# Padding three small SBUF tiles so that matmul operands start at multiples of 512 bytes

## The chip, the cores and the metric

The kernel runs on one core of one Trainium2 chip. The metric is the device time of one execution in microseconds (us). Three runs of the kernel before took 2649.01, 2649.41 and 2650.83 us; their median is 2649.41 us.

## What is computed

The inputs are float32. An attention stage pools `kv` (2 x 384 x 32 x 128) over 4 x 4 blocks, multiplies the pooled rows by `w_sr`, and uses the result (768 rows for each of the 2 batches) as keys and as values for 12288 queries of width 128 in each batch. Two MLPs follow on all 24576 rows, each 128 -> 2048 -> 128.

```
kv_flat = mean_4x4(kv) @ w_sr                  # (2, 768, 128); k = v = kv_flat
s = (q @ k.T) / sqrt(128); s = s - max(s)
x = exp(s) / (sum(exp(s)) + 1e-09) @ v         # (2, 12288, 128) -> 24576 rows
h = x @ moe_w_in;   x = (h * cos(h)) @ moe_w_out                       # MLP 0
h = x @ moe2_w_in;  x = (h / (1 + exp(-1.702 * h))) @ moe2_w_out       # MLP 1
```

## The kernel before

**Products in three parts.** Float32 operands are split in two float32r parts each, a high one and a low one, and a product is made of three matmuls: high by low, high by high, low by high. For the MLPs the helper `mm3` (L107 to L110) issues the three, one line each:

```
def mm3(o, wh, wl, xh, xl, start, stop):
    nc.tensor.matmul(o, wh, xl, start=start, stop=False)      # L108
    nc.tensor.matmul(o, wh, xh, start=False, stop=False)      # L109
    nc.tensor.matmul(o, wl, xh, start=False, stop=stop)       # L110
```

The first operand is the stationary one, which TensorE loads with a weight load of 128 columns (512 bytes of each partition); the second is the moving one, 512 columns (2048 bytes of each partition). Every matmul has a weight load of its own.

**Units and steps.** The 24576 rows are cut in 48 units of 512. In an MLP a unit takes 8 steps. A step expands two blocks of 128 hidden features (`expanded`: six matmuls, moving `xs`, stationary `wi`, into a PSUM tile `w`), makes them non-linear on ScalarE and VectorE (L590 to L603), splits the result into the two parts of `gs` (`split`, L606 to L616), and adds it into the output (`project`: six matmuls, moving `gs`, stationary `wo`, into the PSUM bank `a`, three steps later). Both MLPs together issue 48 x 2 x 8 x 12 = 9216 matmuls of 512 columns.

**Attention.** The first 12 units go through `attn_step`: scores (L388: moving `kT`, stationary `qT`, 384 columns), transposes (L413), and the product with the values (L443: stationary `vN`, 256 columns). The moving operand of L443 is a tile that `pT_place` puts in turn in the place `ph`, in the place `pl`, and in the space of `gs`. The other 36 units go through `burst_step` between the MLP steps: scores at L476 (24 matmuls of 384 columns a unit), and the values at L538 (18 matmuls of 512 columns a unit: stationary `vN`, moving `pl` and `ph`, in the same order of high and low parts as in `mm3`).

**Order of the work.** The order on every engine is written out by hand (`at(step, rank, ...)`, `run`, under `tc.manual_schedule()`). From about 196 us to 440 us only MLP 0 runs, for the first 11 units, and VectorE also prepares the weights of MLP 1 (`w_split`, L227 to L242). From about 490 us to 2350 us each period of 53.14 us holds one unit of MLP 1, one of attention and one of MLP 0. The rest is MLP 1 alone.

**Where tiles lie.** Tiles of a pool lie one behind the other along the partition in the order in which they are made, each rounded up to 32 bytes. Ahead of the first stand 16384 reserved bytes and four constants of 32 bytes, so that the first tile, `ident`, starts at byte 16512. Two tiles of the pool `cp` are much smaller than 512 bytes:

```
peak = cp.tile([P, 2 * B], F32, tag="peak", name="peak")          # L114: 16 bytes, takes 32
half_pi = cp.tile([P, 1], F32, tag="half_pi", name="half_pi")     # L650: 4 bytes, takes 32
```

All tiles made behind each of them in `cp`, and the pools behind `cp`, start 32 bytes further. Within a tile the slices that matmuls read begin at multiples of 512 bytes, so that every operand of a tile has its tile's remainder by 512. The next table gives these remainders, as the built program has them.

Of the kernel before, what the change touches and what calls it, by code (L numbers as in the profile page):

```python
# [11 lines left out]
F32 = mybir.dt.float32  # L12
# [7 lines left out]
P = 128  # L20
# [3 lines left out]
LAG = 3  # L24
T_LAG = 3
BLK = 32
GATE = 1.702
PV_CUTS = (0, 0, 6, 12, 18)
TWO_PI = 2.0 * math.pi
# [6 lines left out]
def tile_pooled_attention_two_mlps(  # L36
# [12 lines left out]
    B, N, C = q.shape  # L49
# [13 lines left out]
    scale = 1.0 / math.sqrt(C)  # L63
    NB, KB = UNIT // BLK, NK // BLK
    assert AHEAD < LEAD < UB and C == P and N % UNIT == 0 and KC * P == NK and HK % P == 0
    assert P // BLK == QT

    cp = ctx.enter_context(tc.tile_pool(name="cp", bufs=1))
# [3 lines left out]
    st = ctx.enter_context(tc.tile_pool(name="st", bufs=4))  # L72
    ps = ctx.enter_context(tc.tile_pool(name="ps", bufs=1, space=bass.MemoryType.PSUM))

    ident = cp.tile([P, P], F32, tag="ident", name="ident")
    make_identity(nc, ident)
    wsr = cp.tile([P, C], F32, tag="wsr", name="wsr")
# [26 lines left out]
    def f32(ap):  # L104
        return ap.bitcast(F32)
# [5 lines left out]


    pooled, staged = {}, {}
    peak = cp.tile([P, 2 * B], F32, tag="peak", name="peak")  # L114

    def kv_place(b, j):

# [197 lines left out]
    def token_blocks(ap, u, i):  # L315

        rows = ap[u * UNIT : (u + 1) * UNIT, i * BLK : (i + 1) * BLK]
        return rows.rearrange("(b j) c -> j b c", j=BLK)

    q_flat = q.rearrange("b n c -> (b n) c")  # L320

    def q_load(u):
# [3 lines left out]
        if u < LEAD:  # L326
            nc.sync.dma_start(t, tokens(q_flat, u))
            return
        t = t.rearrange("p j c -> p (j c)").rearrange("p (b c) -> p b c", c=BLK)
        for i in range(QT):  # L330
            nc.sync.dma_start(t[i * BLK : (i + 1) * BLK], token_blocks(q_flat, u, i))

# [244 lines left out]
    def mlp_step(s, m, u, p):  # L577
# [7 lines left out]
        def nonlinear():  # L585
            h = v["h"]
            g = v["g"] = fp.tile([P, 2, UNIT], F32, tag="f", name=f"g{m}_{u}_{p}")
            if m == 1:

                nc.scalar.activation(g, h, AF.Silu, scale=GATE)  # L590
                return
# [13 lines left out]
        def split():  # L605
            g = v["g"]  # L606
            gs = v["gs"] = gs_ring[turn_of[s] % 3]
            if m == 1:
                nc.scalar.activation(gs[:, 0], g, AF.Copy, scale=1.0 / GATE)  # L609
                nc.vector.scalar_tensor_tensor(  # L610
                    gs[:, 1], g, 1.0 / GATE, f32(gs[:, 0]), op0=ALU.mult, op1=ALU.subtract
                )
# [34 lines left out]
        for i in range(QT):  # L647
            nc.sync.dma_start(token_blocks(out, u, i), r[i * BLK : (i + 1) * BLK])

    half_pi = cp.tile([P, 1], F32, tag="half_pi", name="half_pi")  # L650


    steps = [(attn_step, u, t) for u in range(LEAD) for t in range(QT)]
# [179 lines left out]
```

## Time and profile before

| | before |
|---|---|
| median of three runs | 2649.41 us (2649.01 to 2650.83) |
| profiled execution, its own time | 2649.0 us |
| span from its first to its last instruction | 2647.1 us |
| TensorE (PE) busy | 2607.0 us, 98% of the span |
| VectorE (DVE), ScalarE (ACT), GpSimd (POOL) busy | 78%, 79%, 21% |
| mean granted clock of TensorE | 0.999 |

A matmul's duration in this profile reaches from its start to a modelled end, and the next matmul starts before that end. A busy share of 98% so does not say how fast matmuls follow one another; the distance between two starts says it. The chain of waits cuts its steps at those starts, and a piece of it with a count gives the distance directly.

### The profile page before, as it was taken

To read this page: it belongs to the slowest core of one execution; us is meant where nothing else is said; L and a number is where in the kernel's file an instruction comes from. 1 tells how busy PE (TensorE), PEld (TensorE's weight loads), DVE (VectorE), ACT (ScalarE), POOL (GpSimd) and SP (SyncE) were. 2 spreads that over 40 slices of the span, in tenths; PEclk is the share of its full clock that TensorE was granted. 3 is DMA by queue.
4 is the path that set the end of the run, shared out by engine and by line. 5 is a ranking of instruction groups with operands and counts; after the bars stand their busy time and mean duration, and the time that the engine had idled before them with its cause. 6 is when DMAs were issued, how large, how long until landed. Compare 5 with 4: busy or idle time off the path is not lost.

```text
span 2647.1 us, 32479 instructions
## 1 busy us (share of the span) xinstructions
PE 2607.0 (98%) x11832; PEld 2148.8 (81%) x11832; DVE 2059.2 (78%) x2297; ACT 2101.7 (79%) x2449; POOL 543.9 (21%) x430
## 2 busy tenths in 40 slices
PE   5999999999999999999999999999999999999998
PEld 5987877888888888888888888888888888888887
DVE  6989998878787878787878787878787878765444
ACT  4777788888888888888888888888888888877776
POOL 5842332112111211121111111121112111200000
PEclk9999999999999999999999999999999999999999
DMA  8210001211221122112211221122112211210000
GB/s 216 73 33 16 17 20 28 41 33 32 56 41 33 32 54 43 33 32 51 45 32 32 48 49 33 33 47 49 33 33 44 49 35 32 39 22 9 13 11 16
DMA packets 317434, 105.06 MB, mean 40 GB/s; under 512 B 188112, under 2 KB 309072, under 8 KB 317264
## 3 DMA queue, kind: packets, MB, share of 16 engines
q1 hardware_dynamic: 317264, 102.89, 19.7%
q8 instruction: 95, 1.56, 0.2%
q14 instruction: 75, 0.61, 0.1%
HBM read 33.62 MB, written 12.58 MB: 17 GB/s over the span
## 4 chain that ended last, share of the span: by engine, by line
PE 94%; DVE 4%; DMA 1%; ACT 0%; POOL 0%; issue 0%; SPq 0%; POOLq 0%; DVEq 0%; ACTq 0%
PE a L108 13%; PE w L108 13%; PE w L110 13%; PE w L109 13%; PE a L110 13%; PE a L109 13%; PE a L538 6%; PE w L476 6%; PE a L443 1%; PE w L388 1%; PE w L413 1%; DVE g L603 1%; DMA kv<-in_kv_dram 1%; DVE gs L616 1%; DVE wt L234 0%; DVE nm L395 0%
## 5 line engine op out<-in xcount | busy, mean ns | idle before, releaser
L610 DVE SCALAR_TENSOR_TENSOR gs<-g,gs 128x1024 fp32r<-128x1024 f32 x384 | 469.0, 1222 | 355.8 <-ACT gs L609 355.8
L108 PE MATMUL a<-gs,wo 128*128 128x512 f32 x1536 | 607.9, 396 | 1.2 <-DVE gs L616 0.7
L108 PE MATMUL w<-xs,wi 128*128 128x512 f32 x1536 | 607.6, 396 | 0.6 <-ACT e L489 0.6
L110 PE MATMUL a<-gs,wo 128*128 128x512 f32 x1536 | 607.5, 396 | 0.0
L109 PE MATMUL a<-gs,wo 128*128 128x512 f32 x1536 | 607.5, 395 | 0.0
L109 PE MATMUL w<-xs,wi 128*128 128x512 f32 x1536 | 607.4, 395 | 0.0
L110 PE MATMUL w<-xs,wi 128*128 128x512 f32 x1536 | 607.3, 395 | 0.0
L593 ACT ACTIVATE g<-w,half_pi 128x1024 f32<-128x1024 f32 x384 | 428.4, 1116 | 168.8 <-PE w L110 168.5
L590 ACT ACTIVATE g<-w 128x1024 f32<-128x1024 f32 x384 | 395.2, 1029 | 210.2 <-PE w L110 209.6
L603 DVE TENSOR_TENSOR g<-w,g 128x1024 f32<-128x1024 f32 x384 | 467.9, 1219 | 120.3 <-ACT g L593 116.4
L616 DVE TENSOR_TENSOR gs<-g,gs 128x1024 fp32r<-128x1024 f32 x368 | 451.1, 1226 | 38.3 <-ACT gs L614 36.7
L614 ACT ACTIVATE gs<-g 128x1024 fp32r<-128x1024 f32 x384 | 404.3, 1053 | 2.3 <-DVE g L603 2.3
L609 ACT ACTIVATE gs<-g 128x1024 fp32r<-128x1024 f32 x384 | 399.4, 1052 | 0.0
L377 POOL TENSOR_TENSOR xs<-x,xs 128x512 fp32r<-128x512 f32 x96 | 174.8, 1821 | 859.1 <-PE w L110 444.0
L108 PEld LDWEIGHTS a<-gs,wo 128*128 128x128 f32 x1536 | 288.5, 188 | 72.8 <-DVE gs L616 2.0
L108 PEld LDWEIGHTS w<-xs,wi 128*128 128x128 f32 x1536 | 288.6, 188 | 70.2 <-ACT e L489 0.9
L110 PEld LDWEIGHTS a<-gs,wo 128*128 128x128 f32 x1536 | 288.6, 188 | 69.8
L110 PEld LDWEIGHTS w<-xs,wi 128*128 128x128 f32 x1536 | 288.6, 188 | 69.8
L109 PEld LDWEIGHTS w<-xs,wi 128*128 128x128 f32 x1536 | 288.5, 188 | 69.6
L109 PEld LDWEIGHTS a<-gs,wo 128*128 128x128 f32 x1536 | 288.6, 188 | 69.5
L359 POOL TENSOR_TENSOR qT<-qt,qT 128x512 fp32r<-128x512 f32 x36 | 65.3, 1814 | 708.2 <-ACT qT L358 708.2
L489 ACT ACTIVATE e<-w,nm 128x768 f32<-128x768 f32 x144 | 130.4, 906 | 76.4 <-DVE nm L483 51.5
(98 smaller groups left out, 2582.7 us busy)
## 6 DMA issues: line engine op xcount, KB each, us to landing
pl<-blocks SPq DMA_DIRECT2D x576, 96.0 KB, 2.3
kv<-in_kv_dram SPq DMA_DIRECT2D x48, 256.0 KB, 5.9
out_dram<-r SPq DMA_DIRECT2D x192, 64.0 KB, 2.0
qn<-in_q_dram SPq DMA_DIRECT2D x144, 64.0 KB, 2.3
qn<-in_q_dram SPq DMA_DIRECT2D x12, 256.0 KB, 3.1
raw<-in_moe_w_in_dram SPq DMA_DIRECT2D x8, 256.0 KB, 6.3
x<-in_moe_w_out_dram SPq DMA_DIRECT2D x8, 256.0 KB, 2.9
raws<-in_moe_w_in_dram SPq DMA_DIRECT2D x8, 256.0 KB, 2.7
```

The lines of the kernel that those rows point to most:

```text
L108: nc.tensor.matmul(o, wh, xl, start=start, stop=False)
L109: nc.tensor.matmul(o, wh, xh, start=False, stop=False)
L110: nc.tensor.matmul(o, wl, xh, start=False, stop=stop)
L377: nc.gpsimd.tensor_tensor(d[:, 1], x, f32(d[:, 0]), op=ALU.subtract)
L476: nc.tensor.matmul(sc[:, h, :HK], w, kT[b][:, i, h], start=w is qh and i == 1, stop=w is ql,)
L590: nc.scalar.activation(g, h, AF.Silu, scale=GATE)
L593: nc.scalar.activation(g, h, AF.Sin, bias=half_pi)
L603: nc.vector.tensor_tensor(g, h, g, op=ALU.mult)
L609: nc.scalar.activation(gs[:, 0], g, AF.Copy, scale=1.0 / GATE)
L610: nc.vector.scalar_tensor_tensor(gs[:, 1], g, 1.0 / GATE, f32(gs[:, 0]), op0=ALU.mult, op1=ALU.subtract)
L614: nc.scalar.activation(gs[:, 0], g, AF.Copy)
L616: eng.tensor_tensor(gs[:, 1], g, f32(gs[:, 0]), op=ALU.subtract)
```

## The change

A tile of 384 bytes is made ahead of `ident`, and nothing reads or writes it. `peak` and `half_pi` become tiles of 512 bytes, of which the kernel uses the same columns as before.

```
+LINE = 128
...
+    cp.tile([P, 3 * LINE // 4], F32, tag="pad", name="pad")
     ident = cp.tile([P, P], F32, tag="ident", name="ident")
...
-    peak = cp.tile([P, 2 * B], F32, tag="peak", name="peak")
+    peak = cp.tile([P, LINE], F32, tag="peak", name="peak")[:, : 2 * B]
...
-    half_pi = cp.tile([P, 1], F32, tag="half_pi", name="half_pi")
+    half_pi = cp.tile([P, LINE], F32, tag="half_pi", name="half_pi")[:, :1]
```

The instructions of every engine, their order and their waits are the same before and after; only addresses differ. Start of the operands by their remainder by 512 bytes, in the built programs:

| matmuls | columns | moving, before | stationary, before | both, after |
|---|---|---|---|---|
| L108 to L110, expand | 512 | `xs` 160 | `wi` 192 | 0 |
| L108 to L110, project | 512 | `gs` 160 | `wo` 192 | 0 |
| L538 | 512 | `pl`, `ph` 192 | `vN` 128 | 0 |
| L388, L476 | 384 | `kT` 128 | `qT` 160 | 0 |
| L443 | 256 | `ph`, `pl` 192, or `gs` 160 | `vN` 128 | 0 |
| L339, L413 (transposes) | 128 | `ident` 128 | `qn` 160, `e` 192 | 0 |

One stationary operand stays off a multiple of 512 bytes: the two columns `vr` of the four matmuls at L275 start at a remainder of 64 before and of 384 after.

## Rows read from the trace of the kernel before

**Rows 1.** The page: the span, the busy time of the engines, and in 40 slices of the span the busy tenths of TensorE and its granted clock in tenths.

```profile
span 2647.1 us, 32479 instructions
PE 2607.0 (98%) x11832; PEld 2148.8 (81%) x11832; DVE 2059.2 (78%) x2297; ACT 2101.7 (79%) x2449; POOL 543.9 (21%) x430
...
PE   5999999999999999999999999999999999999998
...
PEclk9999999999999999999999999999999999999999
```

**Rows 2.** Groups of instructions by line and form: TensorE's matmuls of 512 and 384 columns. The columns are the line, engine, operation, output and inputs, shapes and count, then busy us and mean ns of one, then the engine's idle us before them and what ended it.

```profile
L108 PE MATMUL a<-gs,wo 128*128 128x512 f32 x1536 | 607.9, 396 | 1.2 <-DVE gs L616 0.7 <-DVE gs L610 0.5
L108 PE MATMUL w<-xs,wi 128*128 128x512 f32 x1536 | 607.6, 396 | 0.6 <-ACT e L489 0.6
L109 PE MATMUL w<-xs,wi 128*128 128x512 f32 x1536 | 607.4, 395 | 0.0
...
L476 PE MATMUL w<-kT,qT 128*128 128x384 f32 x864 | 168.1, 337 | 0.8 <-ACT e L489 0.8
...
L538 PE MATMUL a<-ph,vN 128*128 128x512 f32 x432 | 134.5, 392 | 0.0
...
L538 PE MATMUL a<-pl,vN 128*128 128x512 f32 x216 | 85.4, 395 | 0.0
...
L388 PE MATMUL w<-kT,qT 128*128 128x384 f32 x288 | 62.4, 352 | 1.3 <-DVE gs L431 1.3
```

**Rows 3.** Windows by stage: the stretch in us, its length, busy us and instructions of PE, PEld, DVE, ACT and POOL, the granted clock, the DMA share and GB/s.

```profile
60.00:196.00 136.00, 132.75 (x959) 126.56 (x958) 121.92 (x244) 101.01 (x180) 93.09 (x92) 1.00 0.22 60
196.00:440.00 244.00, 243.27 (x1041) 195.05 (x1040) 237.67 (x237) 196.40 (x214) 70.75 (x43) 1.00 0.05 16
440.00:490.00 50.00, 48.63 (x214) 39.44 (x213) 39.78 (x44) 42.21 (x49) 7.96 (x7) 1.00 0.23 43
490.00:2350.00 1860.00, 1860.00 (x8192) 1527.23 (x8191) 1479.07 (x1575) 1531.02 (x1750) 320.86 (x245) 1.00 0.22 40
2350.00:2647.00 297.00, 289.61 (x1241) 232.59 (x1239) 142.61 (x124) 207.69 (x217) 22.00 (x12) 1.00 0.07 12
```

**Rows 4.** The chain of waits from 1000 us to 1040 us: the start of a piece in us, its length, and the engine, tile and line (with a count where pieces of one line follow one another). From each of the first six rows to the next is one MLP step of 12 matmuls, so that 60 matmuls lie between the first and the sixth. From the seventh row on a unit of attention follows.

```profile
1002.69 0.23 PE a L110
...
1005.49 0.23 PE a L110
...
1008.29 0.23 PE a L110
...
1011.09 0.23 PE a L110
...
1013.89 0.23 PE a L110
...
1016.69 0.23 PE a L110
...
1022.52 2.09 PE w L476 x12
1024.62 1.39 PE a L538 x6
1026.00 1.05 PE w L476 x6
1027.05 1.39 PE a L538 x6
1028.44 1.05 PE w L476 x6
1029.48 1.39 PE a L538 x6
1030.87 0.24 PE w L108
```

**Rows 5.** The chain of waits from 2345 us to 2362 us: the last product of attention, 18 matmuls of L538 in a row, the one matmul of the MLP behind it, and two more behind that.

```profile
2351.02 4.12 PE a L538 x18
2355.14 0.24 PE w L108
2355.61 0.23 PE w L110
2356.07 0.23 PE w L109
```

**Rows 6.** Timeline of TensorE in the attention stage, 60 to 196 us: start, time from the first start to the modelled end of the ninth matmul, line, output and inputs, shapes and count. All have the stationary operand `vN`; the moving one lies in `gs` or in the places `ph` and `pl` (`pT`).

```profile
60.64 1.22 PE L443 MATMUL a<-gs,vN 128*128 128x256 f32 x9
63.41 1.22 PE L443 MATMUL a<-pT,vN 128*128 128x256 f32 x9
66.25 1.22 PE L443 MATMUL a<-pT,vN 128*128 128x256 f32 x9
...
75.19 1.21 PE L443 MATMUL a<-gs,vN 128*128 128x256 f32 x9
77.97 1.22 PE L443 MATMUL a<-gs,vN 128*128 128x256 f32 x9
```

**Rows 7.** Groups of instructions by line and form: TensorE's weight loads, columns as in the second group.

```profile
L108 PEld LDWEIGHTS w<-xs,wi 128*128 128x128 f32 x1536 | 288.6, 188 | 70.2 <-ACT e L489 0.9 <-DVE g L603 0.2
L110 PEld LDWEIGHTS a<-gs,wo 128*128 128x128 f32 x1536 | 288.6, 188 | 69.8
...
L476 PEld LDWEIGHTS w<-kT,qT 128*128 128x128 f32 x864 | 153.3, 188 | 10.3 <-ACT e L489 1.1
...
L538 PEld LDWEIGHTS a<-ph,vN 128*128 128x128 f32 x432 | 81.1, 188 | 14.5
```

**Rows 8.** Groups of instructions by line and form: VectorE's work on an MLP step, columns as in the second group.

```profile
L610 DVE SCALAR_TENSOR_TENSOR gs<-g,gs 128x1024 fp32r<-128x1024 f32 x384 | 469.0, 1222 | 355.8 <-ACT gs L609 355.8
L603 DVE TENSOR_TENSOR g<-w,g 128x1024 f32<-128x1024 f32 x384 | 467.9, 1219 | 120.3 <-ACT g L593 116.4
L616 DVE TENSOR_TENSOR gs<-g,gs 128x1024 fp32r<-128x1024 f32 x368 | 451.1, 1226 | 38.3 <-ACT gs L614 36.7 <-issue 1.5
```

## The prediction

> **What bounds the kernel now.** I read the page's busy shares first, then the groups by form, the windows by stage, and last the chain of waits for the distance between two matmuls. TensorE is busy for 98% of the span at a granted clock of 0.9 or more in every slice [rows 1]. In the groups its MLP matmuls have almost no idle time before them: 1.2 us for the dearest line, 0.0 for L109 [rows 2]. By stage it is busy for all of the 1860 us from 490 to 2350 us, while VectorE has 1479 and ScalarE 1531 us [rows 3]. So the time is the number of matmuls by the distance from one start to the next, and the change can only matter through that distance. The durations of 395 ns in the groups are not it, since they overlap.
>
> The distances come from the chain. Five MLP steps, 60 matmuls, take 1016.69 - 1002.69 = 14.00 us: 233.3 ns each [rows 4]. Eighteen matmuls of L538 take 4.12 us: 228.9 ns each [rows 5]. Twelve of L476, with 384 columns, take 2.09 us: 174.2 ns [rows 4]. The granted clock is 1.00 in all these stretches [rows 3], which is the level of 2.4 GHz, so that 512 columns alone need 213.3 ns and 384 need 160.0. What a matmul pays above its columns is therefore 20.0 ns in the MLPs, 15.6 at L538 and 14.2 at L476.
>
> That difference is what the forecast rests on. MLP and L538 matmuls have the same shape, the same order of high and low parts, a weight load each, and run in one stream within microseconds of each other, yet one class is 4.4 ns slower. In the program they differ in their addresses. The moving operand starts at a remainder by 512 of 160 in the MLPs (20.0 ns), of 192 at L538 (15.6 ns) and of 128 at L476 (14.2 ns): 32, 64 and 128 are the largest powers of two that divide these, and the extra falls in that order. The stationary remainders (192, 128, 160) give no such order, and a weight load takes 188 ns at each of them [rows 7]. So I read the trace as: a moving operand with a poorly aligned start costs some nanoseconds more.
>
> **The change part by part.** It adds, removes and moves no instruction and no wait; the three tiles cost 1344 bytes of a partition and no time. It does what it says: all operands but `vr` start at 0 by 512, and `vr` serves four matmuls. Four terms follow from the addresses.
>
> *MLP matmuls.* There are 6 x 1536 = 9216 [rows 2]. The bounds are no gain (233.3 ns) and the bare columns (213.3 ns), 20.0 ns below; the nearest row for a better start is L538's 228.9 ns, which I take: 4.4 ns less each. By stage: a period of 53.14 us holds 24 + 18 matmuls of attention, and 1860 / 53.14 is 35 periods, so 8192 - 35 x 42 = 6722 MLP matmuls lie between 490 and 2350 us, 1041 from 196 to 440 us, 1241 - 18 = 1223 after 2350 us [rows 3], and the other 230 around these. 6722 x 4.4 ns = 29.6 us; 1223 x 4.4 = 5.4 us; 230 x 4.4 = 1.0 us.
>
> *The stage from 196 to 440 us* has another limit close by. VectorE is busy there for 237.7 of 244 us [rows 3], and TensorE waits for its `gs`. TensorE could give 1041 x 4.4 ns = 4.6 us, but VectorE has 6.3 us to spare in all and not where it is wanted. I take 3.0 us, between nothing and 4.6.
>
> *Other matmuls.* L538 (648) and the scores (864 + 288) [rows 2] also get better starts. They gain between nothing and all that they pay above their columns, 648 x 15.6 ns + 1152 x 14.2 ns = 26.5 us. As they are the measure for the forecast I take nothing, and keep the upper bound for the range.
>
> *Other engines.* Their operands move too. VectorE's three operations on an MLP step read and write tiles with remainders of 160 and 192 today and take 1222, 1219 and 1226 ns [rows 8], so I see no price of a start there and take nothing. They also stay covered: with 39 us less TensorE still has more work than ScalarE's 1531 of 1860 us.
>
> The sum is 29.6 + 5.4 + 1.0 + 3.0 = 39.0 us. Against the profiled execution's own time of 2649.0 us that gives 2610.0 us; that execution lies 0.4 us below the median of the runs, so I leave it at 2610.
>
> **The rivals.**
>
> *No change.* The start doesn't matter and L538 is faster for another reason, such as where its tiles lie as a whole. For it speaks the one direct comparison in the trace: L443 with the moving operand in `gs` (remainder 160) and in `ph` or `pl` (192), otherwise equal, takes 1.21 to 1.22 us for nine either way [rows 6]. Against it: at 256 columns a matmul is shorter than its weight load of 188 ns [rows 7], which may set the pace and hide a cost on the moving side. The time would be 2649, with 0.2% of it, 5 us, as what a measurement of this kernel can tell from no change. The Trainium skill's page "SBUF — State Buffer" (section "Specifications (TRN2)") speaks for this rival: SBUF lines are 16 bytes long, and what costs is crossing to a new one. By it every start here, a multiple of 32 bytes, is already at a line's start, and the sum would be zero; no run so far shows the line's length.
>
> *More than the forecast.* A start at 0 by 512 is better than any start seen here, and takes off most of the 20.0 ns. At the bare columns the 8175 MLP matmuls outside the VectorE stage give 163.5 us, that stage its 6.3 us, the other matmuls 26.5 us: 2453 us at the very best, and half of the first and none of the last gives 2561. For it: the extra falls with each step of alignment. Against it: from 64 to 128 bytes the step is only 15.6 to 14.2 ns. The skill's page "TensorE: Matmul & The Clock Gate" (section "Back-to-back issue gap") gives N/2.4 + 2.5 ns, 215.8 ns for 512 columns; the trace's 233.3 and 228.9 ns are not that, and by the page 8175 x 17.5 ns = 143 us would go.
>
> *Slower.* Today the moving and the stationary start of a matmul differ: by 32 bytes in the MLPs (160 and 192) and at L476 (128 and 160), by 64 at L538. After the change both are 0 by 512, and if the two reads of TensorE get in each other's way when they begin in step, each matmul pays. The dearest distance in the trace is 0.24 us, the last L538 matmul or the first MLP one at the change of stream [rows 4, 5]: as printed that is between 1.7 and 11.7 ns over 233.3. With 6.7 ns for all 9216 the time is 2649 + 62 = 2711 us, with 1.7 ns 2665. It decides from 0.6 ns a matmul on (5.3 us). Against it: pairs that are 32 apart and 64 apart do equally well in L443 [rows 6], so nothing yet shows that the two starts matter to each other.
>
> **How the numbers follow.** Forecast, MLP matmuls near L538's pace or a few nanoseconds below: 0.50. More than that (below 2570): 0.12. No change: 0.27, above all for L443. Slower: 0.11. Faster is then 0.62, the same 0.27, slower 0.11. The range reaches down to L476's extra of 14.2 ns for all MLP matmuls (8175 x 5.8 ns = 47.4 us, 5 us in the VectorE stage) with the 26.5 us of the others, 2649 - 79 = 2570 us, and up to no change with its 5 us, 2654, rounded to 2655. It leaves out the slower case and most of the larger gain, some 0.2. The forecast alone has 2570 to 2630.
>
> **What would show it.** In the changed kernel's chain 60 MLP matmuls should take 13.7 us instead of 14.00, the 18 of L538 4.12 us or less, and a period 52.3 us instead of 53.14; weight loads should stay at 188 ns. From 196 to 440 us VectorE should be busier than its 97%, and TensorE wait a little more for `gs`. If 60 MLP matmuls still take 14.00 us the start is not the cause, and L538's pace needs another; if they take less but L538 and L476 gain as much, the common part of the extra depends on the start too. If they take more than 14.04 us the two reads collide.

## The result, and the profile after

Four runs of the changed kernel took 2592.68 to 2593.46 us, median 2592.91, beside 2650.01 us for the kernel before (its three runs and a fourth): a ratio of 0.978 (95% interval 0.977 to 0.979), 57 us less. 39 us less were forecast. The lines of the changed kernel stand three further on: L111 to L113 are `mm3`, L479 and L541 the scores and values of the bursts, L446 the values of the attention stage, L606 to L619 VectorE's work on a step.

The page, its span and busy times, as in [rows 1]:

```profile
span 2590.9 us, 32479 instructions
...
PE 2549.7 (98%) x11832; PEld 2147.6 (83%) x11832; DVE 2057.3 (79%) x2297; ACT 2101.2 (81%) x2449; POOL 541.2 (21%) x430
```

The number of instructions and TensorE's busy share are the same, and the other engines' busy times differ by less than 3 us: only TensorE's time is clearly shorter. The chain of waits from 1000 us to 1040 us, to be read as [rows 4]: a unit of attention, and the first `a` matmul of four MLP steps.

```profile
1004.89 2.09 PE w L479 x12
1006.98 1.39 PE a L541 x6
...
1014.61 0.23 PE a L111
...
1017.33 0.23 PE a L111
...
1020.05 0.23 PE a L111
...
1022.77 0.23 PE a L111
```

A step of 12 MLP matmuls takes 2.72 us instead of 2.80: (1022.77 - 1014.61) / 36 is 226.7 ns from start to start, against 233.3 before and 228.9 forecast. Inside the bursts nothing moved: twelve score matmuls take 2.09 us and six of L541 1.39 us, as in [rows 4]. Only the last 18 of L541 do, 4.08 us against 4.12 in [rows 5], also 226.7 ns each.

Where the 56.2 us between the spans came from is read from the first and the last of the following rows, the chain of waits of the whole span, first before, then after:

```profile
491.13 2.09 PE w L476 x12
...
544.26 2.09 PE w L476 x12
```

```profile
486.03 2.09 PE w L479 x12
537.91 2.09 PE w L479 x12
...
2302.19 4.08 PE a L541 x18
```

Up to the first burst shown 491.13 - 486.03 = 5.1 us were won; from there to the last values, which stood at 2351.02 us in [rows 5], 43.7 us, in 35 periods that are 51.88 us long instead of 53.13; and behind them 7.4 us. The windows by stage, as [rows 3]:

```profile
196.00:430.00 234.00, 231.14 (x1011) 188.40 (x1010) 231.58 (x233) 189.75 (x207) 68.87 (x43) 1.00 0.05 16
...
480.00:2300.00 1820.00, 1820.00 (x8209) 1528.90 (x8208) 1481.90 (x1577) 1534.23 (x1754) 320.10 (x245) 1.00 0.18 41
```

In the long stage TensorE still has no gap. In the stage before it VectorE is now busy for 99% instead of 97%, and TensorE, which lacked 0.7 us of 244 before, lacks 2.9 of 234. The waits of TensorE over the span name the cause (us in total, times, longest):

```profile
PE a L111 <- DVE gs L619: 2.9, 5, 0.8
```

How much of the 5.1 us this stage gave is read from TensorE's timeline, from the last 18 values of the attention stage (183 to 190 us) to the first scores of the bursts (430 to 442 us), first before, then after:

```profile
185.87 2.29 PE L443 MATMUL a<-gs,vN 128*128 128x256 f32 x18
...
440.08 2.25 PE L476 MATMUL w<-kT,qT 128*128 128x384 f32 x12
```

```profile
185.27 2.32 PE L446 MATMUL a<-gs,vN 128*128 128x256 f32 x18
...
436.20 3.31 PE L479 MATMUL w<-kT,qT 128*128 128x384 f32 x18
```

The stage takes 254.21 us before and 250.93 after, 3.3 us less. Ahead of it lie 0.6 us of the 5.1, behind it 1.2.

The weight loads, in the groups by form, have not moved, as [rows 7] would have it:

```profile
L112 PEld LDWEIGHTS a<-gs,wo 128*128 128x128 f32 x1536 | 288.4, 188 | 58.9
```

### The profile page after: what moved, and what is told of

The parts are those of the page before. It is cut to its first block, busy times and chain, and to the rows that moved or that the text cites. A ratio compares the mean times of both kernels' runs of the same rounds, so it can differ in the third digit from the quotient of the medians.

```text
span 2590.9 us, 32479 instructions
## 1 busy us (share of the span) xinstructions
PE 2549.7 (98%) x11832; PEld 2147.6 (83%) x11832; DVE 2057.3 (79%) x2297; ACT 2101.2 (81%) x2449; POOL 541.2 (21%) x430
## 4 chain that ended last, share of the span: by engine, by line
PE 88%; DVE 10%; DMA 1%; ACT 0%; issue 0%; SPq 0%; POOL 0%; POOLq 0%; DVEq 0%; ACTq 0%
PE w L111 12%; PE w L112 12%; PE w L113 12%; PE a L111 12%; PE a L113 12%; PE a L112 12%; PE a L541 6%; PE w L479 6%; DVE g L606 3%; DVE gs L619 3%; PE a L446 1%; PE w L391 1%; DVE wt L237 1%; PE w L416 1%; DMA kv<-in_kv_dram 1%; DVE wt L233 1%
## 5 line engine op out<-in xcount | busy, mean ns | idle before, releaser
L111 PE MATMUL a<-gs,wo 128*128 128x512 f32 x1536 | 599.0, 390 | 3.5 <-DVE gs L619 2.9
L111 PE MATMUL w<-xs,wi 128*128 128x512 f32 x1536 | 598.1, 389 | 0.6 <-ACT e L492 0.6
L112 PE MATMUL w<-xs,wi 128*128 128x512 f32 x1536 | 598.0, 389 | 0.0
L113 PE MATMUL a<-gs,wo 128*128 128x512 f32 x1536 | 597.9, 389 | 0.0
L113 PE MATMUL w<-xs,wi 128*128 128x512 f32 x1536 | 597.9, 389 | 0.0
L112 PE MATMUL a<-gs,wo 128*128 128x512 f32 x1536 | 597.7, 389 | 0.0
L606 DVE TENSOR_TENSOR g<-w,g 128x1024 f32<-128x1024 f32 x384 | 467.8, 1218 | 103.7 <-ACT g L596 102.8
L619 DVE TENSOR_TENSOR gs<-g,gs 128x1024 fp32r<-128x1024 f32 x368 | 452.5, 1230 | 27.0 <-ACT gs L617 25.4
L111 PEld LDWEIGHTS a<-gs,wo 128*128 128x128 f32 x1536 | 288.3, 188 | 67.6 <-DVE gs L619 6.4
L111 PEld LDWEIGHTS w<-xs,wi 128*128 128x128 f32 x1536 | 288.3, 188 | 61.2 <-ACT e L492 0.9
L113 PEld LDWEIGHTS a<-gs,wo 128*128 128x128 f32 x1536 | 288.3, 188 | 60.1
L113 PEld LDWEIGHTS w<-xs,wi 128*128 128x128 f32 x1536 | 288.3, 188 | 59.9
L499 POOL TENSOR_SCALAR e<-e,rs 128x768 f32<-128x768 f32 x144 | 131.1, 911 | 283.5 <-DVE rs L498 234.3
```

What stands on the lines that cost most here:

```text
L606: nc.vector.tensor_tensor(g, h, g, op=ALU.mult)
L619: eng.tensor_tensor(gs[:, 1], g, f32(gs[:, 0]), op=ALU.subtract)
```

## The experiments

Each diff is against the changed kernel. "Apart" is the stationary start less the moving start of an MLP matmul. Three theories were on the table: M, the moving operand's start matters; S, the stationary one's does; R, the two must agree.

### One part of the change at a time

`e1_pad_only` (MLP moving at 32 by 512 bytes, stationary at 64), with 

> Only the unread tile ahead of `ident` is kept; `peak` and `half_pi` are small again. MLP matmuls: moving starts at 32 by 512, stationary at 64; L538: moving 64, stationary 0. Theory M (the start of the moving operand by 64 bytes sets the distance): the MLPs stay at 233 ns, the time is 2649 us within 5, L538's 18 in a row take 4.08 us as after the change. Theory S (the start of the stationary operand by 64 bytes): stationary at 64 is good, 227 ns, 2593 us. Theory R (both must have the same remainder): not the same, so 231 to 235 ns and 2635 to 2670 us.

`e2_moving_only` (0 and 32), with 

> `half_pi` is small again, the other two tiles are padded: MLP moving starts at 0 by 512, stationary at 32; L538 moving at 32, stationary at 0. Theory M: MLPs at 227 ns as with the whole change, 2593 us, L538's 18 in a row at 233 ns (4.20 us). Theory S: MLPs at 233 ns, 2645 to 2650 us, L538 at 227 ns (4.08 us). Theory R: both as slow as before or slower, 2649 us or more.

`e3_stationary_only` (32 and 0), with 

> `peak` is small again and `half_pi` takes 480 bytes: MLP moving starts at 32 by 512, stationary at 0; L538 both at 0. Theory M: MLPs at 233 ns, 2645 to 2650 us, L538's 18 in a row 4.08 us. Theory S: MLPs at 227 ns, 2593 us. Theory R: MLPs at 233 ns, 2645 to 2650 us; it differs from M in the kernel with moving at 0 and stationary at 32.

```
e1: peak = cp.tile([P, 4], ...)      half_pi = cp.tile([P, 1], ...)
e2:                                  half_pi = cp.tile([P, 1], ...)
e3: peak = cp.tile([P, 4], ...)      half_pi = cp.tile([P, 120], ...)
```

All three give back the whole gain: 2650.19, 2650.92 and 2649.12 us, ratios to the kernel before of 1.000 (0.999 to 1.001), 1.001 (1.000 to 1.002) and 1.000 (0.999 to 1.001). The chain of waits of each, two starts of a period and the last values, e1 first:

```profile
969.97 2.09 PE w L479 x12
1023.11 2.09 PE w L479 x12
...
2351.60 4.12 PE a L541 x18
```

```profile
970.48 2.10 PE w L479 x12
1023.65 2.10 PE w L479 x12
...
2352.99 4.20 PE a L541 x18
```

```profile
968.71 2.09 PE w L479 x12
1021.85 2.09 PE w L479 x12
...
2350.52 4.11 PE a L541 x18
```

The periods are 53.14, 53.17 and 53.14 us, those of the kernel before. A perfect moving start with the stationary one 32 bytes off (e2) is worth nothing, and so is the reverse (e3). M and S both fall: M, on which the prediction stood, had 2593 us for e2. R had the three times right. One row doesn't fit R by itself: in e3 both starts of L541 are at 0, and its 18 take 4.11 us instead of 4.08. In the trace its first six starts are 230.7 ns apart and the other twelve 226.7, so the pace of starts that agree came only after some matmuls, behind MLP matmuls whose starts do not agree.

### All operands at 64, and all at 32

`e4_all_64`, with 

> All three tiles padded, and the first by 64 bytes more, so that every operand starts at 64 by 512 instead of 0. If 64 bytes are the unit that counts (theories M, S and R alike): 227 ns, 2593 us within 4. If the unit is 128, 256 or 512 bytes: MLPs at 229 to 233 ns, as L538 was before at 192 by 512, and 2610 to 2650 us.

`e5_all_32`, with 

> All three tiles padded, the first by 32 bytes more: every operand starts at 32 by 512, so that no start is a multiple of 64 but moving and stationary agree. Theory R (what counts is that the two starts agree): MLPs at 226.7 ns, 2593 us within 4. Theory A (each of the two starts must be a multiple of 64 bytes for itself, and one that is not costs the whole amount): MLPs at 233 ns or more, 2650 us or more.

```
e4: cp.tile([P, 112], F32, tag="pad", name="pad")      # 448 bytes instead of 384
e5: cp.tile([P, 104], F32, tag="pad", name="pad")      # 416 bytes
```

2594.07 us (0.979, 0.978 to 0.981) and 2594.61 us (0.979, 0.978 to 0.981): as fast as at 0. Chain of waits of e5:

```profile
954.89 2.11 PE w L479 x12
1006.79 2.11 PE w L479 x12
...
2304.22 4.08 PE a L541 x18
```

The period is 51.90 us and the last values take 4.08 us, although no operand starts at a multiple of 64 bytes. The start by itself doesn't matter, down to the 32 bytes by which tiles can be placed; what matters is that the two starts agree. The title's multiple of 512 is one way to make them agree.

### How far apart they may be

`e6_apart_64`, with 

> `half_pi` takes 64 bytes: MLP moving starts at 0, stationary at 64, so both are multiples of 64 and 64 apart; L538 has moving at 64 and stationary at 0. Theory R by 512 bytes: the MLPs take L538's pace of before, 229.0 ns, 9216 x 2.3 ns = 21 us more than with the whole change, 2614 us. Theory A, and R by 64 bytes: 226.7 ns, 2593 us; but then L538's 229 ns in the kernel before, and with the first tile alone, has no cause.

`e7_apart_128`, with 

> `half_pi` takes 128 bytes: MLP moving starts at 0, stationary at 128. If the unit by which the two starts must agree is 128 bytes or less: MLPs at 226.7 ns, 2593 us. If it is 256 or 512 bytes: between 226.7 and 229 ns, up to 2614 us.

`e8_apart_256`, with 

> `half_pi` takes 256 bytes: MLP moving starts at 0, stationary at 256. If the unit by which the two starts must agree is 256 bytes or less: MLPs at 226.7 ns, 2593 us. If it is 512 bytes: above 226.7 ns and above 2597 us.

`r11_apart_16`, with 

> The whole change, and the four weight tiles begin 16 bytes into a place that is a multiple of 512 bytes: MLP moving starts at 0, stationary at 16; L538 has both at 0. If every disagreement that is no multiple of 256 bytes costs the same, as 32, 64 and 128 bytes did: MLPs at 233.3 ns, 2650 us. If the unit below is 32 bytes, so that 16 falls within it: 226.7 ns, 2593 us. L538's last 18 settle at 226.7 ns either way.

```
e6, e7, e8: half_pi = cp.tile([P, 16 or 32 or 64], ...)      # 64, 128, 256 bytes
r11:  t = cp.tile([P, 2 * DFF + LINE], ...)                   # for wi, and likewise wo
      wi[m] = t[:, 4 : 4 + 2 * DFF].rearrange("p (i x) -> p i x", i=2)
```

| kernel | apart | time, us | ratio to before (95%) |
|---|---|---|---|
| r11 | 16 | 2641.21 | 0.997 (0.996 to 0.998) |
| e6 | 64 | 2650.31 | 1.000 (0.999 to 1.001) |
| e7 | 128 | 2650.64 | 1.001 (1.000 to 1.002) |
| e8 | 256 | 2593.28 | 0.979 (0.977 to 0.981) |

Chain of waits of e6, e7 and e8:

```profile
968.64 2.10 PE w L479 x12
1021.80 2.10 PE w L479 x12
...
2350.80 4.20 PE a L541 x18
```

```profile
968.29 2.09 PE w L479 x12
1021.47 2.09 PE w L479 x12
...
2350.96 4.20 PE a L541 x18
```

```profile
954.82 2.11 PE w L479 x12
1006.72 2.11 PE w L479 x12
```

64 and 128 bytes apart the period is 53.16 and 53.18 us, 256 apart 51.90: 0 and 256 bytes keep the gain, 32, 64 and 128 lose it, so the unit is 256 bytes. The expectation for e6, that 64 apart would cost as much as at L538 before (229.0 ns), missed; it costs the full 233.3. And L541 in e6, moving at 64 and stationary at 0, takes 4.20 us for its 18, where the very same starts took 4.12 in e1. So apart from a multiple of 256 the two starts alone don't settle the distance.

`r11` shows how this can be. Its chain of waits from 1040 us to 1056 us, and from 2346 us to 2366 us:

```profile
1048.58 0.24 PE a L111
...
1051.38 0.24 PE a L111
```

```profile
2351.02 4.08 PE a L543 x18
...
2356.46 0.23 PE a L111
...
2359.18 0.23 PE a L111
```

In the periods its steps take 2.80 us, as if 16 bytes were 32. Behind the last 18 values, whose starts agree, the same MLP matmuls take 2.72 us a step. 16 bytes apart both distances occur.

A run of values is not the only thing that the change of pace follows. In r11's timeline of TensorE from 332.5 to 350 us, in the stage of MLP 0 alone, these two rows are 60 matmuls apart:

```profile
334.24 0.39 PE L111 MATMUL a<-gs,wo 128*128 128x512 f32 x1
...
347.84 0.39 PE L111 MATMUL a<-gs,wo 128*128 128x512 f32 x1
```

They take 13.60 us, 226.7 ns each. Up to 333.5 us the trace has 233 ns; TensorE had waited 158 ns at 330.65 us, and after a late matmul at 349.88 us the 233 ns return. So the same matmuls at the same starts change their pace in the middle of a stream, here near interruptions, and then keep it; what sets it is not shown.

The tail behind the last values, some 1220 matmuls by 6.6 ns or 8 us, is the 8 us by which r11 is faster than the kernel before.

### Values in a row in the bursts

`r9_pv_in_a_row`, with 

> The whole change, and in the bursts the 18 matmuls of attention's values stand in a row (PV_CUTS 0, 0, 0, 0, 18) instead of three sixes between scores. With the change six of them take 231.5 ns each although their starts agree, and the 18 in a row at the end 226.6. Theory T (after other matmuls it takes some five matmuls until the distance settles at 226.7 ns): in the bursts the 18 take about 227 to 229 ns each, and 35 x 18 x 3 to 4.5 ns = 2 to 3 us go, 2590 to 2591 us. Theory L (something in the bursts slows them): 231.5 ns, 2593 us.

```
-PV_CUTS = (0, 0, 6, 12, 18)
+PV_CUTS = (0, 0, 0, 0, 18)
```

2647.78 us (0.999, 0.998 to 1.000): the whole gain is lost, which neither theory said. Chain of waits, then TensorE's waits (us in total, times, longest):

```profile
1026.17 4.12 PE a L541 x18
...
1079.66 4.12 PE a L541 x18
```

```profile
PE w L479 <- ACT e L492: 49.0, 36, 1.4
```

On the distance theory T was right: the 18 take 4.12 us, 228.9 ns each, where six took 1.39 us, 231.7. In the burst at 1026 us the first nine of them are 231.1 ns apart in the trace and the other nine 226.7. But between the scores the sixes had covered the time in which ScalarE frees the score buffers; without them TensorE waits 1.4 us for it in each of 36 bursts, which is most of the 1.6 us by which the period, 53.49 us, is longer than with the change.

### VectorE's stage

`r10_more_eased`, with 

> The whole change, and from 196 to 430 us GpSimd takes 16 more of the subtractions of L619 from VectorE (two of each five steps instead of one). Theory V (VectorE kept back a part of the gain in that stage): its busy share falls from 99% to near 91%, TensorE no longer waits for `gs`, and the first burst starts 3 to 8 us earlier: 2585 to 2590 us. Rival P (GpSimd's 2.4 us for one, or the two engines' shared work, holds `gs` up as long): 2593 us or more.

`r12_eased_three`, with 

> The whole change, and from 196 to 430 us GpSimd takes three of each five subtractions of L619. With two of five the first burst started at 432.1 us instead of 436.2. If VectorE still holds the stage: it starts at 428 to 431 us, 2587 to 2589 us. If GpSimd's 2.4 us each, or VectorE's waits for the port that both use, are the limit now: no earlier than 432 us, 2590 us or more.

```
-                eased.add(step)
+                eased.update((step, step + 2))              # r10
+                eased.update((step, step + 2, step + 4))    # r12
```

r10 takes 2590.41 us (0.977, 0.976 to 0.979), r12 2593.71 us (0.979, 0.978 to 0.980). The window of the stage and the first long piece of the chain in r10, and the window in r12:

```profile
196.00:430.00 234.00, 232.70 (x1024) 191.49 (x1023) 218.81 (x218) 192.61 (x209) 108.97 (x59) 1.00 0.06 16
```

```profile
481.94 2.08 PE w L479 x12
```

```profile
196.00:430.00 234.00, 230.13 (x1007) 187.63 (x1006) 223.82 (x202) 188.08 (x205) 143.57 (x73) 1.00 0.06 16
```

With 16 more subtractions on GpSimd VectorE falls to 218.8 of 234 us (93.5%, where theory V had 91), TensorE works through 1024 matmuls in the window instead of 1011, and the burst that began at 486.03 us begins at 481.94, 4.1 us earlier. Not all of that is the edit's: the last 18 values of the attention stage, ahead of the first moved subtraction, already start 1.2 us earlier than in the changed kernel. The same stretch of r10's timeline as shown above for the changed kernel:

```profile
184.04 2.31 PE L446 MATMUL a<-gs,vN 128*128 128x256 f32 x18
...
432.11 3.31 PE L479 MATMUL w<-kT,qT 128*128 128x384 f32 x18
```

The stage takes 248.07 us instead of 250.93, 2.9 us less; in e4, e5, e8 and r9, where nothing of it was edited and the starts agree, it takes 251.05 to 251.12. So VectorE did hold back part of the gain. r10 is the fastest version measured, by 2.5 us in the medians, though the intervals of the two ratios overlap; its 2590.41 us lie just above theory V's 2585 to 2590. With another 16 the gain is gone, as the rival had it: in r12 the stage takes 252.05 us. In that window of r12 an operation of VectorE of 256 columns, 419 ns long on average in the changed kernel (about 280 in 14 of 16), takes

```profile
L230 DVE TENSOR_SCALAR wt<-raws 128x256 uint32<-128x256 uint32 x16 | 34.8, 2177 | 0.0
```

on average, about as long as one subtraction on GpSimd (2.4 us). In the trace 15 of the 16 begin 0.15 to 1.05 us behind the start of such a subtraction and end 0.15 us behind its end; the other has none beside it and takes 286 ns. VectorE has 16 operations fewer than in r10 and is busy for longer: its subtractions take 18.5 us less, the five operations that prepare weights (L230 to L245) 22 us more, 85.0 instead of 63.0.

## Why the prediction was right, and where it was not

- **What bounds the kernel.** Right. The gain came through the distance between matmul starts, and the other engines' busy times hardly changed.
- **The step that failed** is "So I read the trace as: a moving operand with a poorly aligned start costs some nanoseconds more". The order 32, 64, 128 of the largest powers of two fitted three classes by chance: e2 has the best moving start and no gain, e5 a poor one and the whole gain. What counts instead is the difference of the two starts: 226.7 ns where it is 0 or 256 bytes, 233.3 where it is 32, 64 or 128. In the three classes that were compared, moving and stationary starts were 32, 64 and 32 bytes apart, all in disagreement. That the time still fell into the forecast's range is luck: the change put the moving starts at 0 and made the two starts agree at once, and by the forecast's mechanism e2 would have had the gain too.
- **The size of the MLP term.** 4.4 ns were taken, 6.6 measured (233.3 to 226.7). L538 was not an example of well placed operands, only another class whose starts disagree, which happened to run at 228.9 ns. With 6.6 ns the 6722 matmuls give 44.4 us against 43.7 measured from 490 to 2350 us (29.6 forecast), and the 1223 behind 8.1 us against 7.4 (5.4 forecast).
- **VectorE's stage.** Right, and near in size, though the 3.0 us were a choice between nothing and 4.6: 3.3 us were won in it, where its matmuls by 6.6 ns would give some 7, and r10 got 2.9 us more out of it. Up to the burst at 491 us 5.1 us were won in all (4.0 forecast).
- **Other matmuls.** Nothing was taken and next to nothing came: scores 2.09 us, sixes of L541 1.39 us as before, only the last 18 0.04 us less. The upper bound of 26.5 us was far off. L446 was a little slower, nine in 1.23 us instead of 1.22 [rows 6]; over the stage its starts are 118.8 ns apart in the trace instead of 117.4:

```profile
60.12 1.23 PE L446 MATMUL a<-gs,vN 128*128 128x256 f32 x9
62.90 1.23 PE L446 MATMUL a<-pT,vN 128*128 128x256 f32 x9
```

- **No change.** Its evidence, L443 with equal times at remainders of 160 and 192, was true and read rightly as undecided. By the result both had starts that disagree with `vN` (32 and 64 bytes), and agreement brought them nothing either; why 256 columns differ from 512 in this stays open. The reason given against this evidence, that the weight load of 188 ns may set the pace there, does not fit its own rows: nine matmuls with a weight load each in 1.22 us are at most 136 ns apiece. The sum of zero that the prediction drew from the 16-byte lines in the Trainium skill's page "SBUF — State Buffer" (section "Specifications (TRN2)") missed 57 us. The lines themselves are not contradicted, since the cost lies between two starts and not at one; no run here shows them.
- **More than the forecast.** The result lies in the forecast's own 2570 to 2630 us, above this rival's 2570. Of the 20.0 ns above the columns 6.6 went, not most, and e5 shows that it was not the alignment by itself. 13.3 ns remain above the columns' 213.3; no run here held a pace below 226.7 ns. The 2.5 ns of "TensorE: Matmul & The Clock Gate" (section "Back-to-back issue gap") in the Trainium skill stand there for an isolated matmul, which no run here measures, and not for a stream with a weight load each, so that the prediction's 143 us do not follow from what is stated there.
- **Slower.** The rival said that the two reads of TensorE matter to each other, and by that it was closer to the mechanism than the forecast, but its sign was wrong: starts that agree are the good case. Why they are was not measured. That the weight load, which in the trace starts 2 to 4 ns behind each matmul (around 1015 us, before and after), and the moving read get in each other's way when their starts differ is an argument that fits, not something shown.

## What to carry to other kernels

When TensorE streams without gaps, compare the distance between matmul starts across classes of the same shape; a difference of some nanoseconds may come from where the tiles lie. Here, for float32r matmuls of 512 columns, moving and stationary starts had to agree modulo 256 bytes (0, 16, 32, 64, 128 and 256 bytes apart were tried), and one small tile between two large ones broke that for all behind it. Two or three classes that line up with one property are not evidence for it if a second property (here the difference of two starts) varies with them: a kernel that sets one and not the other costs one run.

## What the runs showed of the hardware

- Matmuls of 512 columns, float32r, a weight load each, at a granted clock of 1.00: 226.7 ns from start to start with the two starts equal modulo 256 bytes (both 0, both 32, both 64, or 256 apart), 233.3 ns in the MLP steps with 32, 64 or 128 bytes between them.
- Where the starts disagree they alone don't set the distance: 16 bytes apart gave 2.80 us a step in the periods and 2.72 us behind the last 18 values and from 334 to 348 us, in the stage of MLP 0; L541 with moving at 64 and stationary at 0 took 4.12 us in one kernel and 4.20 us in another. What sets it is open.
- With starts that agree, sixes of L541 between scores still take 231.7 ns and 18 in a row behind scores 228.9, those behind MLP matmuls 226.7 (in e3, whose MLP starts disagree, only from the seventh on). Scores of 384 columns gained nothing; values of 256 columns were 1.4 ns slower in the changed kernel.
- Small operations of VectorE can take as long as GpSimd's operation beside them: 2177 ns on average (r12) instead of 280 without one, for 256 columns.
